# Attention and gated convolution FFN on one core: the last batch's copies get buffers of their own, and some twenty entries of the hand-written order move

## The chip, the cores and the metric

The kernel runs on one core of a Trainium2 chip. The metric is the device time of one execution in microseconds (us). Before the change it is 247.61 us, the median of three runs (248.05, 246.43 and 247.61).

The core has five engines that run side by side: TensorE (PE; its weight loads are shown as PEld), VectorE (DVE), ScalarE (ACT), GpSimd (POOL) and SyncE (SP). Matmuls write into PSUM, which DVE and ACT read; everything else lies in SBUF. Transfers are issued on the queues of SP or ACT and run on 16 DMA engines that all queues share.

## The reference

Eight batches of eight heads of causal attention, 576 positions of width 64, with a decay made of the running sum of logarithms; its output, 576 x 512 for each batch, goes through a feed-forward network of width 1024 whose hidden layer is gated by a convolution of three taps over the positions.

```python
def attn(q, k, v, f):                       # 8, 8, 576, 64; f: 8, 8, 576
    scores = q @ k.transpose(0, 1, 3, 2) / 8.0
    cum = np.cumsum(np.log(np.clip(f, 1e-4, 1.0)), axis=-1)
    scores = np.where(causal, -1e9, scores + cum[..., :, None] - cum[..., None, :])
    return softmax(scores) @ v

def ffn(x, w_in, conv_w, w_out):            # x: 8, 576, 512
    h = np.maximum(x @ w_in, 0.0)           # 8, 576, 1024
    gate = sigmoid(three_tap_conv_over_positions(h, conv_w))
    return (h * gate) @ w_out               # 8, 576, 512, float32
```

## The kernel before

**Tiling.** Attention works on half batches: hb 0 to 15, four heads each. For one hb the scores come in diagonal blocks (`sd`, two per hb), off-diagonal strips (`so`) and the last 64 positions (`st`). ACT turns each into exponentials (`ed`, `eo`, `et`), PE multiplies them by v (`pv`), DVE divides by the row sums (`n`, `m`), and the result is transposed (`t`, `tx`). After two half batches, batch b goes through the FFN in eight chunks ff of 128 hidden columns: `f` is the first matmul, `r` the ReLU on ACT, `c` and `d` the convolution on DVE, `a` the gate's function on ACT, `g` its product on DVE. The second matmul is `o`; `e` copies its PSUM tile into SBUF and `s` stores it.

**The last batch's output.** For b = 7 the second matmul is split by ff: `o7.c.ff` is one 128 x 128 by 128 x 512 matmul for position chunk c (0 to 4, of 128 positions). The last one for c is `o7.c.7`. Chunks 0 and 1 are the two halves of one PSUM tile of 128 x 1024, 2 and 3 the halves of another, 4 has a third. `e7.c` copies chunk c (line 485 before), `s7.c` stores it (line 491; chunk 4 in two pieces, lines 500 and 501). The copies of 0 and 1 go into the two halves of one SBUF tile `ob`, those of 2 and 3 into those of another, and the second of each pair is declared to come behind the first.

**The start.** The first two half batches are loaded plainly (`ld`) and transposed on PE (`tp`); `cl` then writes the transposed tile from PSUM to SBUF, on ACT or DVE. The others are loaded by transposing transfers (`q2.0` is q of half batch 2, `q2.1` its k). `ki` stores the decay rows to DRAM in three transfers, and `rw1`, `rw2` read some of them back into rows of the q and k tiles (lines 203 and 204, two small transfers each); the scores of that half batch wait for them. `wi0` to `wi3` load quarters of the first weight matrix (512 KB each), `wo0` to `wo3` those of the second, and `wic`, `woc` cast them. `v` loads values, `va` casts them. `cw` is a transpose of the convolution weights into PSUM, and `cwt` is seven small DVE instructions that read it (lines 298 to 305).

**What sets the order.** One list, `ORDER`, names every task, with `@` and an engine where there is a choice. `Plan.play` walks it and issues each task in turn, so each engine and each queue executes its own tasks in list order. Buffers are handed out in the same walk: `free[r].pop(0)` for a taker, `append` at the giver. There are four PSUM tiles (`ps`, numbered 129 to 132 in the program), so where in the list a task gives its tile back also decides which tile the later ones get. The recording layer adds the waits between engines. Each engine runs its instructions strictly in order, so that one that waits holds what stands behind it.

Of the kernel before, what the change touches and what calls it, by code (L numbers as in the profile page):

```python
# [21 lines left out]
class Plan:  # L22
# [34 lines left out]
def kernel(  # L57
# [11 lines left out]
    nc = tc.nc  # L69
# [36 lines left out]
    cw = cpool.tile([128, NFF, 3], FP32, name="cw")  # L106
    cwt = cpool.tile([128, NFF, 3], FP32, name="cwt")
# [316 lines left out]
    outf = out.rearrange("b s c -> (b s) c")  # L424
# [26 lines left out]
    def tanh(b, ff):  # L451
        nc.scalar.activation(hg_of(b, ff), u_t[slot[f"c{b}.{ff}", "u"]], AF.Sigmoid if (b, ff) in LATE else AF.Tanh, scale=cw[:, ff, 1:2])  # L452
# [11 lines left out]
    def shift(b):  # L464
        return 0 if low(b) == (b % 2 == 0) else S - 512
# [16 lines left out]
    def evac_chunk(b, c, e):  # L482
        j = c % 2
        o, i = ob_t[slot[f"e{b}.{c & ~1}", "ob"]][:, j, :], ps_of(f"o{b}.{c & ~1}.0")[:, 512 * j:512 * j + 512]
        (nc.scalar.copy if e == "ACT" else nc.vector.tensor_copy)(o, i)

    def store_chunk(b, c):
        if c == 4:
            return store(f"e{b}.4", b, c)
        r = b * S + shift(b) + 128 * c  # L490
        nc.sync.dma_start(outf[r:r + 128, :], ob_t[slot[f"e{b}.{c & ~1}", "ob"]][:, c % 2, :])

    def store(ev, b, c):
        ob, r = ob_t[slot[ev, "ob"]], b * S + shift(b) + 128 * c
        if c < 4:
            nc.sync.dma_start(outf[r:r + 256, :].rearrange("(j p) c -> p j c", p=128), ob)
        elif shift(b):
            nc.sync.dma_start(outf[b * S - SL:b * S + SL, :], ob[:, 0, :])
        else:
            nc.sync.dma_start(outf[b * S + 512:(b + 1) * S, :], ob[0:SL, 0, :])  # L500
            nc.sync.dma_start(outf[(b - 1) * S:(b - 1) * S + SL, :], ob[SL:128, 0, :])
# [35 lines left out]
    for hb in range(NHB):  # L537
        b = hb // 2
# [3 lines left out]
        if hb < NPL:  # L542
# [40 lines left out]
        for p in range(2):  # L583
            i = 2 * hb + p
# [34 lines left out]
    for b in range(B):  # L619
        last = b == B - 1  # L620
        for ff in range(NFF):
            add(f"f{b}.{ff}", "PE", [f"tx{2 * b}", f"tx{2 * b + 1}"] + [f"wic{2 * (ff // 4) + j}" for j in range(2)],
                lambda b=b, ff=ff: ffn1(b, ff), take=["ps"], behind=[f"f{b}.{ff - 1}"] if ff else [],
                give=[("xt", f"tx{2 * b}")] if ff == NFF - 1 else [])
            add(f"r{b}.{ff}", "ACT", [f"f{b}.{ff}"], lambda b=b, ff=ff: relu(b, ff), take=["ht"], give=[("ps", f"f{b}.{ff}")])
            add(f"c{b}.{ff}", "DVE", [f"r{b}.{ff}", "cwt"], lambda b=b, ff=ff: conv(b, ff, 0), take=["u"])
            add(f"d{b}.{ff}", "DVE", [f"c{b}.{ff}"], lambda b=b, ff=ff: conv(b, ff, 1))
            if ff == 0:
                add(f"h{b}", "ACT", [f"d{b}.{ff}"], lambda: None, take=["ho" if b % 2 else "he"])
            add(f"a{b}.{ff}", "ACT", [f"d{b}.{ff}"] + (["sgt"] if (b, ff) in LATE else []), lambda b=b, ff=ff: tanh(b, ff), give=[("u", f"c{b}.{ff}")],  # L630
                behind=[f"h{b}"])
            add(f"g{b}.{ff}", "DVE", [f"a{b}.{ff}"], lambda b=b, ff=ff: gate(b, ff), give=[("ht", f"r{b}.{ff}")])
        wo = [f"woc{j}" for j in range(4)]
        before = [f"g{b - 1}.{ff}" for ff in range(NFF)]
        if last:
            for ff in range(NFF):
                for c in range(NKB):
                    add(f"o{b}.{c}.{ff}", "PE", [f"g{b}.{ff}"] + (before if c == 4 and ff == 0 else []) + (wo if ff == 0 else []),
                        lambda b=b, c=c, ff=ff: ffn2(b, f"o{b}.{c & ~1}.0", c, [ff]),
                        take=["ps"] if ff == 0 and c % 2 == 0 else [],  # L640
                        behind=[f"o{b}.{c}.{ff - 1}"] if ff else [f"o{b}.{c - 1}.0"] if c % 2 else [])
        else:
            for c in range(4 + b % 2):
                a = c // 2
                first = f"o{b}.{2 * a}"
                add(f"o{b}.{c}", "PE", [f"g{b}.{ff}" for ff in range(NFF)] + (before if c == 4 else []) + wo,
                    lambda b=b, c=c, first=first: ffn2(b, first, c, range(NFF)), take=["ps"] if c % 2 == 0 else [],
                    behind=[f"o{b}.{c - 1}"] if c else [], give=[("he", f"h{b - 1}"), ("ho", f"h{b}")] if c == 4 else [])
        if last:
            for c in range(NKB):  # L650
                add(f"e{b}.{c}", "ACT/DVE", [f"o{b}.{c}.{NFF - 1}"], lambda e, b=b, c=c: evac_chunk(b, c, e),
                    take=["ob"] if c % 2 == 0 else [], behind=[f"e{b}.{c - 1}"] if c % 2 else [])
                add(f"s{b}.{c}", "SP", [f"e{b}.{c}"], lambda b=b, c=c: store_chunk(b, c))
            continue
        for a in range(2 + b % 2):
# [36 lines left out]
```

## Time and profile before

| | |
|---|---|
| median of three runs | 247.61 us (246.43 to 248.05) |
| the profiled execution | 246.53 us |
| its span, from the first to the last instruction | 244.8 us |
| PE busy | 226.9 us, 93% of the span |
| ACT, DVE, POOL busy | 206.8, 205.9, 51.5 us |
| granted TensorE clock | 0.999 of full speed |
| moved by DMA | 49.68 MB, 203 GB/s on average |

The span of the profiled execution is 1.73 us shorter than its own time. Busy shares are averages; PE's row also counts a modelled end for each matmul, and matmuls overlap. In the rows of the timeline the columns are start, duration, engine, line, operation, output and inputs, shapes and count, and in brackets how long the engine was idle before and what ended that. "SPq" and "ACTq" are the engines' issuing of transfers, not the transfers themselves.

### The profile page before, as it was taken

What the parts mean: (1) busy time and instruction counts of PE and PEld (TensorE: products, weight loads), DVE (VectorE), ACT (ScalarE), POOL (GpSimd) and SP (SyncE); (2) the same over time, 40 slices, a digit from 0 to 9 for tenths busy, and PEclk for the clock granted to TensorE, in tenths of its full rate; (3) what the DMA queues carried; (4) which work ended last, traced back from release to release, by engine and by line L of the source; (5) the groups of instructions that cost most, each with busy time, mean ns of one, the idle gap of its engine ahead of it and who ended that gap; (6) DMA issues with size and microseconds to landing.
All of it is one profiled execution on the core that took longest, in us unless ns stands there. A gap on an engine that the chain in (4) does not pass through costs nothing.

```text
span 244.8 us, 6395 instructions
## 1 busy us (share of the span) xinstructions
PE 226.9 (93%) x2627; PEld 145.2 (59%) x2627; DVE 205.9 (84%) x323; ACT 206.8 (84%) x278; POOL 51.5 (21%) x77
## 2 busy tenths in 40 slices
PE   0899799779989999999999999999999999999991
PEld 0787585557555676575556765685575566444440
DVE  5635359999998999999999979996999889999941
ACT  2768677999989899999999999999988996798442
POOL 8020520004220030022311580165302221000000
PEclk9999999999999999999999999999999999999999
DMA  7999999999899999999999999969997870541426
GB/s 189 333 162 243 289 212 197 196 249 260 187 178 177 222 162 246 252 297 208 195 251 264 202 189 274 263 144 186 240 255 192 210 165 3 146 162 58 163 86 214
DMA packets 120280, 49.68 MB, mean 203 GB/s; under 512 B 109863, under 2 KB 110375, under 8 KB 120251
## 3 DMA queue, kind: packets, MB, share of 16 engines
q1 hardware_dynamic: 120085, 48.97, 89.7%
q8 instruction: 20, 0.33, 0.6%
q10 hardware_dynamic: 166, 0.31, 0.4%
q14 instruction: 9, 0.07, 0.1%
HBM read 21.11 MB, written 10.17 MB: 128 GB/s over the span
## 4 chain that ended last, share of the span: by engine, by line
PE 80%; DVE 8%; DMA 6%; issue 1%; ACT 1%; POOL 1%; ACTq 1%; SPq 0%; DVEq 0%
PE ps L475 25%; PE ps L430 21%; PE ps L313 15%; PE ps L390 7%; PE ps L395 3%; PE ps L166 2%; PE ps L415 2%; PE ps L321 2%; DMA pd<-in_moe_conv_w_dram 2%; DMA ob<-in_moe_w_out_dram 2%; DVE u L447 2%; DVE u L449 2%; DMA qk<-image 2%; DVE hg L459 1%; DVE qk L186 1%
## 5 line engine op out<-in xcount | busy, mean ns | idle before, releaser
L430 PE MATMUL ps<-xt,w_in_f 128*128 128x512 f16 (+1 forms) x512 | 69.9, 286 | 0.0
L371 ACT ACTIVATE pp<-ps 128x1024 f16<-128x1024 f32 x64 | 64.8, 1033 | 4.4 <-PE ps L313 2.8
L475 PE MATMUL ps<-w_out_f,hg 128*128 128x512 f16 x288 | 66.9, 379 | 0.7 <-POOL w_out_f L519 0.7
L313 PE MATMUL ps<-qk 128*128 128x128 bf16 (+2 forms) x576 | 63.4, 240 | 1.6 <-DMA qk<-image 0.8
L447 DVE SCALAR_TENSOR_TENSOR u<-ht,cwt 128x576 f32<-128x576 f16 x64 | 53.3, 849 | 3.2 <-ACT ht L441 3.2
L452 ACT ACTIVATE hg<-u,cw 128x576 f16<-128x576 f32 x64 | 48.7, 784 | 5.9 <-DVE u L449 5.8
L449 DVE SCALAR_TENSOR_TENSOR u<-ht,cwt,u 128x576 f32<-128x576 f16 x64 | 53.1, 844 | 0.5
L430 PEld LDWEIGHTS <-w_in_f 128*128 128x128 f16 x512 | 34.4, 98 | 28.5
L313 PEld LDWEIGHTS <-qk 128*128 128x128 bf16 x576 | 39.2, 98 | 19.8 <-issue 3.0
L441 ACT ACTIVATE ht<-ps 128x576 f16<-128x576 f32 x64 | 40.9, 663 | 6.2 <-DVE hg L459 3.1
L475 PEld LDWEIGHTS <-hg 128*128 128x128 f16 x288 | 26.9, 98 | 29.7 <-issue 0.9
L459 DVE SCALAR_TENSOR_TENSOR hg<-hg,ht 128x576 f16<-128x576 f16 x51 | 39.0, 776 | 0.5 <-ACT hg L452 0.5
L357 POOL TENSOR_SCALAR_AFFINE_SELECT pp<-pd 128x1024 f16<-128x1024 f32 x16 | 19.7, 1244 | 51.7 <-ACT pd L354 51.7
L390 PE MATMUL ps<-va,pp 128*128 128x65 f16 x640 | 24.8, 193 | 1.0 <-DVE va L218 1.0
L390 PEld LDWEIGHTS <-pp 128*128 128x128 f16 x640 | 22.5, 97 | 3.5 <-DVE va L218 1.3
L406 DVE TENSOR_TENSOR xm<-ps,rc 128x896 f16<-128x896 f32 (+1 forms) x32 | 23.9, 751 | 0.5
L354 ACT ACTIVATE pp<-ps 128x1024 f16<-128x1024 f32 x16 | 16.6, 1038 | 5.2 <-PE ps L313 4.2
L354 ACT ACTIVATE pd<-ps 128x1024 f32<-128x1024 f32 x16 | 16.2, 1023 | 1.2 <-PE ps L313 1.0
L218 POOL CAST va<-vf 128x1024 f16<-128x1024 f32 x8 | 9.3, 1168 | 33.2 <-PE ps L415 18.5
L321 PE MATMUL ps<-mask,ident 128*128 128x512 bf16 (+1 forms) x40 | 14.3, 358 | 1.6 <-ACT pp L371 0.8
L404 DVE RECIPROCAL rc<-ps 128x14 f32<-128x14 f32 (+1 forms) x32 | 6.7, 209 | 9.8 <-PE ps L395 5.9
L480 ACT COPY ob<-ps 128x1024 f32<-128x1024 f32 (+1 forms) x14 | 12.9, 919 | 0.3 <-issue 0.2
(83 smaller groups left out, 176.2 us busy)
## 6 DMA issues: line engine op xcount, KB each, us to landing
vf<-in_v_dram SPq DMA_DIRECT2D x32, 256.0 KB
out_dram<-ob SPq DMA_DIRECT2D x14, 512.0 KB
qk<-blank SPq DMA_DIRECT2D x8, 432.0 KB
ob<-in_moe_w_in_dram SPq DMA_DIRECT2D x4, 512.0 KB
ob<-in_moe_w_out_dram SPq DMA_DIRECT2D x4, 512.0 KB
out_dram<-ob SPq DMA_DIRECT2D x6, 256.0 KB
vf<-in_v_dram SPq DMA_DIRECT2D x8, 128.0 KB
qk<-blank SPq DMA_DIRECT2D x8, 108.0 KB
```

The costliest lines, as they stand in the source:

```text
L313: nc.tensor.matmul(o, tk[:, h * S + k0:h * S + k0 + 128], tq[:, h * S + q0:h * S + q0 + n], start=first, stop=last and not by_matmul(hb, h))
L354: nc.scalar.activation(o, ps_of(f"sd{i}").rearrange("p (s c) -> p s c", s=2), AF.Exp, scale=SCALE)
L371: nc.scalar.activation(pair(i)[:, s, 512:1536], ps_of(f"so{i}.{s}"), AF.Exp, scale=SCALE)
L390: nc.tensor.matmul(ps[:, c:c + D + 1], block(hb, h, m, n), va[:, h, m, 0:D + 1], start=(m == 0), stop=(m == n))
L406: nc.vector.tensor_tensor(xm[:, CUT * D * u:CUT * D * u + nj * k * D].rearrange("p (j x d) -> p j x d", x=k, d=D), got[:, :, :, 0:D], r.un ...
L430: nc.tensor.matmul(ps[:, t0:t1], w_in_f16[:, cc, 128 * ff:128 * (ff + 1)], xt[:, cc // 2, x:x + t1 - t0], start=(cc == 0), stop=(cc == NCC ...
L441: nc.scalar.activation(ht_of(b, ff)[:, 2:2 + S], ps_of(f"f{b}.{ff}")[:, 0:S], AF.Relu, scale=1.0 if (b, ff) in LATE else 0.5)
L447: nc.vector.scalar_tensor_tensor(u, ht[:, 1:1 + S], cwt[:, ff, 0:1], ht[:, 2:2 + S], op0=ALU.mult, op1=ALU.add)
L449: nc.vector.scalar_tensor_tensor(u, ht[:, 3:3 + S], cwt[:, ff, 1:2], u, op0=ALU.mult, op1=ALU.add)
L452: nc.scalar.activation(hg_of(b, ff), u_t[slot[f"c{b}.{ff}", "u"]], AF.Sigmoid if (b, ff) in LATE else AF.Tanh, scale=cw[:, ff, 1:2])
L459: nc.vector.scalar_tensor_tensor(hv, hv, 1.0, ht_of(b, ff)[:, 2:2 + S], op0=ALU.add, op1=ALU.mult)
L475: nc.tensor.matmul(ps[:, 512 * (c % 2):512 * (c % 2 + 1)], w, w_out_f16[:, ff, :], start=(ff == 0), stop=(ff == NFF - 1))
```

## The change

There are two parts.

**The last batch's tail.** Chunks 1 and 3 are now copied into tiles of the pool `u`, which the convolution used; chunks 0, 2 and 4 keep an `ob` tile each. The declared order between the copies of a pair is gone. The store of chunk 2 is issued from ACT's queue instead of SP's. Chunk 0's copy is cut in two: `e7.0` copies columns 0 to 255 and a new task `eh7.0` columns 256 to 511, and its store waits for both.

**The order.** `q2.1` goes behind `ki`, and `wi3` moves ahead of both q2 loads. `cwt` goes from the start to a place behind `eo1.0`. Within q5 and within q6 the k load now precedes the q load. In the middle, `sd19`, `d3.4`, `r4.7`, `o4.1` and `d6.1` go a few places later in the list, and `va8.1` moves from DVE to POOL. At the end `o7.0.4` moves behind `o7.1.7` and `o7.1.7` ahead of `o7.0.5`, `e7.3` stands behind `o7.3.7` and `e7.1` behind `o7.0.4`. DVE copies chunks 4, 3 and 1 and the second half of 0, ACT copies 2 and the first half of 0; before, DVE copied 4 and 3 and ACT 2, 0 and 1.

```diff
-dca cw ld0 ... v0.4 va0.0@POOL va0.1@POOL q2.1 ki@SP cl0.0.0@ACT cl0.0.1@ACT cl0.1.0@ACT tp0.1.1 q2.0 cwt sd0 ed0 cl0.1.1@DVE wi1 wic1@POOL ... so1.0 st0 eo1.0 pv0.0
+dca cw ld0 ... v0.4 va0.0@POOL va0.1@POOL ki cl0.0.0@ACT cl0.0.1@ACT cl0.1.0@ACT tp0.1.1 wi3 q2.0 sd0 ed0 q2.1 cl0.1.1@DVE wi1 wic1@POOL ... so1.0 st0 eo1.0 cwt pv0.0
...
+    def last_out(b, c):
+        return u_t[slot[f"e{b}.{c}", "u"]] if c % 2 else ob_t[slot[f"e{b}.{c}", "ob"]][:, 0, :]
+
-    def evac_chunk(b, c, e):
-        j = c % 2
-        o, i = ob_t[slot[f"e{b}.{c & ~1}", "ob"]][:, j, :], ps_of(f"o{b}.{c & ~1}.0")[:, 512 * j:512 * j + 512]
+    def evac_chunk(b, c, e, n0=0, n1=512):
+        o, i = last_out(b, c)[:, n0:n1], ps_of(f"o{b}.{c & ~1}.0")[:, 512 * (c % 2) + n0:512 * (c % 2) + n1]
         (nc.scalar.copy if e == "ACT" else nc.vector.tensor_copy)(o, i)
...
-        nc.sync.dma_start(outf[r:r + 128, :], ob_t[slot[f"e{b}.{c & ~1}", "ob"]][:, c % 2, :])
+        (nc.scalar if c == 2 else nc.sync).dma_start(outf[r:r + 128, :], last_out(b, c)[:, 0:D_MODEL])
...
             for c in range(NKB):
-                add(f"e{b}.{c}", "ACT/DVE", [f"o{b}.{c}.{NFF - 1}"], lambda e, b=b, c=c: evac_chunk(b, c, e),
-                    take=["ob"] if c % 2 == 0 else [], behind=[f"e{b}.{c - 1}"] if c % 2 else [])
-                add(f"s{b}.{c}", "SP", [f"e{b}.{c}"], lambda b=b, c=c: store_chunk(b, c))
+                half = 256 if c == 0 else 512
+                add(f"e{b}.{c}", "ACT/DVE", [f"o{b}.{c}.{NFF - 1}"], lambda e, b=b, c=c, half=half: evac_chunk(b, c, e, 0, half),
+                    take=["u" if c % 2 else "ob"])
+                if c == 0:
+                    add(f"eh{b}.{c}", "ACT/DVE", [f"o{b}.{c}.{NFF - 1}"], lambda e, b=b, c=c: evac_chunk(b, c, e, 256, 512),
+                        behind=[f"e{b}.{c}"])
+                add(f"s{b}.{c}", "ACT" if c == 2 else "SP", [f"e{b}.{c}"] + ([f"eh{b}.{c}"] if c == 0 else []), lambda b=b, c=c: store_chunk(b, c))
```

What stands in the program after these edits is shown at three places.

First, SP's queue near the start, from the last load of the first values on; `qk_87` is the tile of half batch 2, `qk_86` that of half batch 1, and the `image` rows that write `qk` are `rw1` and `rw2`. Before:

```order
L210 DMA vf_89<-in_v_dram 64x8x64
L180 DMA_TRANSPOSE qk_87<-in_k_dram 128x2304
L280 DMA image<-kc 64x576 x3
L180 DMA_TRANSPOSE qk_87<-in_q_dram 128x2304
L511 DMA ob_125<-in_moe_w_in_dram 128x2x512
L203 DMA qk_86<-image 1x2304
L204 DMA qk_86<-image 2x2304
L511 DMA ob_126<-in_moe_w_in_dram 128x2x512
```

and after:

```order
L210 DMA vf_89<-in_v_dram 64x8x64
L280 DMA image<-kc 64x576 x3
L513 DMA ob_125<-in_moe_w_in_dram 128x2x512
L180 DMA_TRANSPOSE qk_87<-in_q_dram 128x2304
L180 DMA_TRANSPOSE qk_87<-in_k_dram 128x2304
L513 DMA ob_126<-in_moe_w_in_dram 128x2x512
L203 DMA qk_86<-image 1x2304
L204 DMA qk_86<-image 2x2304
```

The k transpose stands behind the three `image` stores, and one weight load more stands ahead of `rw1`.

Second, ACT's instructions on the PSUM tiles in the same stretch, with the tile's number: `ed0`, `eo0.1`, `eo0.0`, `cl1.0.0`, `ed1`, `cl1.1.1`, `eo1.1`. Before:

```order
L354 ACTIVATE pp0_95<-ps2_131 128x2x512
L371 ACTIVATE pp0_95<-ps3_132 128x1024
L371 ACTIVATE pp0_95<-ps2_131 128x1024
L172 ACTIVATE qk1_86<-ps0_129,lim_76 128x1152
L354 ACTIVATE pp1_96<-ps3_132 128x2x512
L172 ACTIVATE qk1_86<-ps0_129,lim_76 128x1152
L371 ACTIVATE pp1_96<-ps1_130 128x1024
```

and after:

```order
L354 ACTIVATE pp0_95<-ps2_131 128x2x512
L371 ACTIVATE pp0_95<-ps3_132 128x1024
L371 ACTIVATE pp0_95<-ps1_130 128x1024
L172 ACTIVATE qk1_86<-ps2_131,lim_76 128x1152
L354 ACTIVATE pp1_96<-ps1_130 128x2x512
L172 ACTIVATE qk1_86<-ps3_132,lim_76 128x1152
L371 ACTIVATE pp1_96<-ps1_130 128x1024
```

Tile 129, which `cw` holds until `cwt`, is not among them any more: the work turns on three tiles, and `ed1` (the fifth row) reads the tile that `eo0.0` (the third row) read, where before it read the one of `eo0.1` (the second row).

Third, the end of PE's queue with the waits that the recording layer put there: `o7.3.7`, `o7.2.7`, `o7.1.6`, `o7.1.7`, `o7.0.4`, `o7.0.5`, each with its weight load; tile 130 holds chunks 2 and 3, tile 132 chunks 0 and 1. After the change:

```order
L475 MATMUL ps1_130<-w_out_f16_70,hg_124 128x512
L475 LDWEIGHTS hg_124
L475 MATMUL ps1_130<-w_out_f16_70,hg_124 128x512 [waits DVE_49]
L475 LDWEIGHTS hg_124
L475 MATMUL ps3_132<-w_out_f16_70,hg_124 128x512
L475 LDWEIGHTS hg_124
L475 MATMUL ps3_132<-w_out_f16_70,hg_124 128x512
L475 LDWEIGHTS hg_124
L475 MATMUL ps3_132<-w_out_f16_70,hg_124 128x512
L475 LDWEIGHTS hg_124
L475 MATMUL ps3_132<-w_out_f16_70,hg_124 128x512 [waits DVE_49]
```

and DVE's copies of the chunks (4, 3, 1 and the half of 0), after:

```order
L487 COPY ob0_125<-ps0_129 128x512 [waits DMAHW6_49,DMAHW4_49,PE_49]
L487 COPY u2_122<-ps1_130 128x512 [waits PE_49]
L487 COPY u1_121<-ps3_132 128x512 [waits DVE_49,PE_49]
L487 COPY ob2_127<-ps3_132 128x256 [waits DMAHW7_49,DMAHW1_49,Activation_49]
L693 UNCONDITIONAL_BRANCH
```

where before there were two (4 and 3):

```order
L457 TENSOR_TENSOR hg_124<-hg_124,ht0_115 128x576 [waits PE_49,Activation_49]
L457 TENSOR_TENSOR hg_124<-hg_124,ht1_116 128x576 [waits PE_49]
L485 COPY ob3_128<-ps0_129 128x512 [waits DMAHW6_49,DMAHW4_49,PE_49]
L485 COPY ob2_127<-ps3_132 128x512 [waits DMAHW6_49,Activation_49]
L687 UNCONDITIONAL_BRANCH
```

In the list after the change `e7.3` stands ahead of `o7.2.7` and `e7.1` ahead of `o7.0.5`, and those two matmuls, which write the other half of the tile that the copy reads, wait for DVE. Before, no matmul behind `o7.4.7` waits for anything. The wait of chunk 3's copy for ACT is gone, and the half copy of chunk 0 waits for ACT.

2 lines of the change are left out of this document (1 added, 1 removed).

## The prediction

> **What bounds the kernel now.** I read first a table by stage: the busy time of each engine in four stretches, with the DMA share and rate in the last two columns.
>
> ```profile
> 8.20:25.00 16.80, 16.80 (x212) 14.31 (x213) 9.60 (x16) 13.60 (x13) 1.37 (x2) 1.00 1.15 239
> 25.00:71.00 46.00, 40.72 (x548) 27.55 (x545) 37.93 (x57) 40.40 (x55) 11.32 (x11) 1.00 1.06 226
> 71.00:239.60 168.60, 168.44 (x1866) 102.40 (x1865) 153.87 (x232) 149.37 (x207) 33.42 (x34) 1.00 0.85 192
> 239.60:244.80 5.20, 0.07 (x1) 0.00 (x0) 0.38 (x1) 1.07 (x2) 0.00 (x0) 0.94 0.70 235
> ```
>
> The columns after the length are PE, PEld, DVE, ACT, POOL, granted clock. From 71.0 to 239.6 PE is busy for 168.44 of 168.60 us at the full clock. Nothing can be won there by moving other engines' work; an edit can only open a gap. From 25 to 71 PE idles for 46.0 - 40.7 = 5.3 us, and 5.2 us follow the last matmul. So the two ends decide. The waits of PE between, from the list of who waited for whom, and four pieces of the chain that ended last:
>
> ```profile
> PE ps L390 <- DVE va L218: 1.0, 1, 1.0
> PE ps L313 <- DMA qk<-image: 0.8, 1, 0.8
> PE ps L475 <- POOL w_out_f L519: 0.7, 1, 0.7
> ```
>
> ```profile
> 22.51 3.80 DMA qk<-image
> 26.36 0.40 PE ps L313 x4
> ...
> 64.27 5.08 DMA ob<-in_moe_w_out_dram
> 69.40 1.70 POOL w_out_f L519
> ```
>
> PE's first wait on the way is 0.8 us for `rw1`, the small read behind a full DMA queue that lands 3.80 us after its issue at 22.51; its last is 0.7 us for a weight cast whose load landed late, before 71.1.
>
> **The tail, step by step.** The last six matmuls and the four copies around them, then the three rows that price a half copy and a restart of PE:
>
> ```profile
> 238.21 1.46 PE L475 MATMUL ps<-w_out_f,hg 128*128 128x512 f16 x6
> ...
> 237.33 0.69 DVE L485 COPY ob<-ps 128x512 f32<-128x512 f32 x1 [2.10 <-PE ps L475]
> 238.67 0.58 ACT L485 COPY ob<-ps 128x512 f32<-128x512 f32 x1 [3.40 <-issue]
> 239.28 0.69 DVE L485 COPY ob<-ps 128x512 f32<-128x512 f32 x1 [1.26 <-ACT ob L485]
> 239.70 1.07 ACT L485 COPY ob<-ps 128x512 f32<-128x512 f32 x2 [0.45 <-PE ps L475]
> ```
>
> ```profile
> L475 PE MATMUL ps<-w_out_f,hg 128*128 128x512 f16 x288 | 66.9, 379 | 0.7 <-POOL w_out_f L519 0.7
> 24.40 0.38 ACT L333 ACTIVATE pt<-ps 128x256 f16<-128x256 f32 x1 [0.33 <-PE ps L318]
> 32.09 0.42 DVE L406 TENSOR_TENSOR xm<-ps,rc 128x256 f16<-128x256 f32 x1
> 27.23 1.02 ACT L354 ACTIVATE pp<-ps 128x1024 f16<-128x1024 f32 x1 [2.44 <-PE ps L313]
> 28.31 0.60 PE L313 MATMUL ps<-qk 128*128 128x64 bf16 x4 [0.45 <-ACT pp L354]
> ```
>
> Matmuls start every (1.46 - 0.38) / 5 = 0.216 us; the first of the six is `o7.2.7`, at 238.21, the last `o7.0.7`, at 239.29. The copies that wait for them start 0.46 and 0.41 us later (238.67, 239.70); I take 0.42. PE starts again 28.31 - 28.25 = 0.06 us after an ACT instruction that held it. Chunk 4's copy at 237.33 puts `o7.4.7` at 236.91.
>
> What goes: chunk 3's copy no longer waits for chunk 2's (1.26 us), chunk 1's no longer follows chunk 0's on ACT. What comes are waits of PE for DVE, at `o7.2.7` and `o7.0.5`; behind each stands all that PE has left. In the new order:
> - `o7.3.7` is the fourth after `o7.4.7`: 236.91 + 4 x 0.216 = 237.77. `e7.3` runs from 238.19 to 238.88. `o7.2.7`, due at 237.99, starts at 238.94: 0.95 us lost.
> - `e7.2` on ACT from 239.36 to 239.94; its store is issued there.
> - `o7.1.6`, `o7.1.7`, `o7.0.4` at 239.16, 239.37, 239.59. `e7.1`, which waits for PE, runs from 240.01 to 240.70. `o7.0.5`, due at 239.80, starts at 240.76: 0.96 us lost. `o7.0.7` starts at 241.19, 1.9 us later than before.
> - The half copy `e7.0` at 241.61, 0.38 us, to 241.99; then `eh7.0` on DVE, which waits for ACT, 0.42 us, to 242.47. Its store is issued at 242.50.
>
> The halves cost 0.06 + 0.38 + 0.42 = 0.86 us in a row, where one copy takes 0.58. [...]
>
> Before, the last store was issued at 240.9, and the rates show when the data had left, against a store that stood alone:
>
> ```profile
> L491 SPq DMA_DIRECT2D out_dram<-ob x4: 351/409/524, 239.3 to 240.9; - x4
> L496 SPq DMA_DIRECT2D out_dram<-ob x1: 372/372/372, 235.3 to 235.3; - x1
> ```
>
> ```profile
> 236.00:237.00 1.00, 1.00 (x6) 0.48 (x5) 0.00 (x0) 0.00 (x0) 0.00 (x0) 1.00 0.82 309
> 237.00:238.00 1.00, 1.00 (x7) 0.41 (x6) 0.67 (x1) 0.00 (x0) 0.00 (x0) 1.00 0.58 215
> 241.00:242.00 1.00, 0.00 (x0) 0.00 (x0) 0.00 (x0) 0.00 (x0) 0.00 (x0) 1.00 0.92 342
> 242.00:243.00 1.00, 0.00 (x0) 0.00 (x0) 0.00 (x0) 0.00 (x0) 0.00 (x0) 1.00 1.04 385
> 243.00:244.00 1.00, 0.00 (x0) 0.00 (x0) 0.00 (x0) 0.00 (x0) 0.00 (x0) 1.00 0.35 131
> ```
>
> The stores queued at 385 GB/s until 243 + 131 / 385 = 243.35, 2.4 us after the last issue. The lone store of 524 KB, issued at 235.3, moved 309 KB before 237, so at that rate it began 0.8 us before 237, at 236.2: 0.9 us after its issue. Now the last 262 KB stand alone: 242.50 + 0.9 + 262 / 385 = 244.1, which is 0.75 us later. If a first byte takes 1.2 us, it is 1.05. The row nearest is the lone store; since the last one also has ACT's store ahead of it I take **+0.9**. Bounds: +0.3 (the halves overlap, 0.48 less) and +1.05.
>
> **The head.** `cwt` now keeps its PSUM tile, so `sd1` takes the tile that `eo0.0` reads.
>
> ```profile
> 17.45 0.38 PE L321 MATMUL ps<-mask,ident 128*128 128x512 bf16 x1
> ...
> 17.15 1.02 ACT L371 ACTIVATE pp<-ps 128x1024 f16<-128x1024 f32 x1 [0.79 <-PE ps L318]
> 18.07 1.30 ACT L172 ACTIVATE qk<-ps,lim 128x1152 uint16<-128x1152 uint16 x1
> 19.42 1.02 ACT L354 ACTIVATE pp<-ps 128x1024 f16<-128x1024 f32 x1
> 20.43 1.31 ACT L172 ACTIVATE qk<-ps,lim 128x1152 uint16<-128x1152 uint16 x1
> ```
>
> `sd1` started at 17.45; it now waits for 18.17 + 0.06: 0.78 us. `ed1` (19.42) then starts near 20.2 and `cl1.1.1`, on which `rw1` waits, ends near 22.5 instead of 21.74. `so1.1` waits for `ed1` another 0.25 us, so PE comes to `sd2` about 1.0 us later, where 0.94 us of idle time (its wait of 0.8 with the matmul ahead of it) stood: at 26.45 against 26.36. The seven instructions of `cwt`, 1.3 us, now lie between DVE's casts:
>
> ```profile
> 10.47 0.18 DVE L298 COPY cw<-ps 128x24 f32<-128x24 f32 x1
> 11.63 0.17 DVE L305 TENSOR_TENSOR cwt<-cw,cwt 128x8 f32<-128x8 f32 x1
> 19.05 0.28 DVE L220 CAST va<-vf 64x256 f16<-64x256 f32 x1
> 20.00 1.48 DVE L174 TENSOR_SCALAR qk<-ps,lim 128x1152 uint16<-128x1152 uint16 x1 [0.68 <-PE ps L166]
> ```
>
> From 19.33 to 20.65 they stand ahead of `cl1.1.0` (20.00), which PE, 0.78 us late, holds to 20.8 in any case; it ends at 22.3, before 22.5: nothing more. Then `rw1` needs its landing. `wi3`, 524 KB, now stands ahead of it: at the stage's 226 GB/s 2.3 us. Against that, DMA engines were nearly idle where `q2.1` stood:
>
> ```profile
> 17.00:18.00 1.00, 1.00 (x18) 0.88 (x16) 0.34 (x1) 0.85 (x1) 0.83 (x2) 1.00 0.07 7
> 20.00:21.00 1.00, 1.00 (x15) 0.71 (x12) 1.00 (x1) 1.00 (x2) 0.00 (x0) 1.00 0.60 132
> ```
>
> 7 and 132 KB instead of 226 are 1.4 us of room. If `wi3` fills it, `rw1` lands 2.3 - 1.4 = 0.9 us later; the bounds are 0 (PE is late anyway) and 2.3. I take 0.9. The bytes up to `wo2` are the same, so that load is not later, and the 0.7 us for which PE waited for it take up most: **+0.2** at 71 us, between -0.7 (no wait left there) and 2.3 - 0.7 = +1.6.
>
> **The middle.** The swaps within q5 and q6 exchange equal transfers; `sd19`, `o4.1`, `d3.4`, `r4.7`, `d6.1` change places with work that PE has queued; `va8.1` takes one small cast (0.28 us in the row at 19.05) off DVE. PE is full there, so 0; a gap that one opens would be as long as the matmul group displaced, which I leave to the range.
>
> **Sum.** 246.53 + 0.9 + 0.2 = 247.6 us for the profiled execution. The median of the runs is 247.61, 1.1 above it, so the forecast is **248.6 us**.
>
> **Rivals.**
> - Slower: `wi3` fills no hole, and `rw1` lands the full 2.3 us later. It decides from 0.8 us on, where PE's slack at 70 us ends. For it: the hole lies where a transposing load had just been issued, and these loads still stand there. Against: the two loads are now back to back. Time: 247.61 + 0.9 + 1.6 = 250.1. Chance 0.13.
> - Faster: the stream of transfers moves up by its 1.4 us of holes, and the waits of 1.0 (value cast) and 0.7 (weight cast) go. For it: in 8 to 71 us DMA is the fullest resource (1.15, 1.06). Against: the cast on DVE stood in a queue of DVE work, not for a transfer. 247.61 + 0.9 - 1.7 = 246.8. Chance 0.2.
> - The two matmuls do not wait long, because DVE comes sooner than I think. Then `e7.1` runs from 239.06, `e7.0` from 239.70, the last half ends at 240.6 and the stores, no longer in one bunch, end about 0.3 us sooner: 247.61 - 0.3 + 0.2 = 247.5. Against it: each copy can start only when its own last matmul is done. Chance 0.15.
> - My forecast: 0.52. That the copies still wait for each other, against the words of the change, is part of it.
>
> **Chances.** About 1% (2.5 us) is what a measurement of this kernel can tell from no change; the runs shown spread over 1.6. Below 245.1 no case reaches by itself: 0.05. Above 250.1: half of the first rival and the upper end of the forecast, 0.11. Within: 0.84. The range for 8 in 10 goes from the faster rival to the slower one, 246.8 to 250.1.
>
> **What would show it.** Right: two gaps of PE of about 0.95 us among the last nine matmuls, each ended by a DVE copy; the half copy on DVE behind ACT's; the last store issued about 1.3 us after `o7.0.7` starts, with no queue ahead of it; a wait of PE of 0.8 us near 17.5 and `sd2` between 26.4 and 27.3. Wrong: no gap at the tail; `rw1` landing past 27.5; a wait of PE between 71 and 237 us; or a PE that reaches 71 us work more than 0.7 us early.

## The result, and the profile after

The changed kernel takes 248.68 us (median of 22 runs, 247.42 to 251.38) against 247.24 us for the kernel before in as many (245.69 to 249.23). The ratio is 1.0064, with a 95% interval from 1.0040 to 1.0088: 1.6 us slower, with an interval from 1.0 to 2.2. The ratios, here and below, leave out executions that lie more than 1.5% above the fastest of their kernel (here the one of 251.38), so that they differ a little from the ratio of the medians. The forecast was 248.6 us, within 0.1 us of the median, and the measured time lies in its range. The profiled execution is one of the longest: 250.91 us, span 249.2, 4.4 us longer than that of before. Its trace shows what goes wrong, but too large for the median. Experiments 2 and 4 have the same start, experiment 7 the same but for `cwt`; their traced executions (247.04, 246.57 and 246.64 us) are among the quicker ones of their kernels, and PE waits 1.46, 0.91 and 1.35 us for `rw1` in them. An execution near the median was not traced.

The longest wait of PE in the changed kernel is the one at its very start, 7.0 us (7.3 before). The next two in the list (total, times, longest) stood at 0.8 us and nowhere before:

```profile
PE ps L313 <- DMA qk<-image: 3.4, 1, 3.4
PE ps L475 <- DVE u L487: 1.6, 2, 0.8
```

The first is the wait for `rw1`, the second the two at the tail. The weight cast `woc2`, for which PE waited 0.7 us near 70 us before, is not in the list.

**The tail.** The end of the timeline of the changed kernel:

```profile
236.64 5.34 PE L475 MATMUL ps<-w_out_f,hg 128*128 128x512 f16 x24
...
242.02 0.69 DVE L487 COPY u<-ps 128x512 f32<-128x512 f32 x1 [0.17 <-PE ps L475]
...
242.77 1.02 PE L475 MATMUL ps<-w_out_f,hg 128*128 128x512 f16 x4 [0.78 <-DVE u L487]
...
243.83 0.69 DVE L487 COPY u<-ps 128x512 f32<-128x512 f32 x1 [1.11 <-PE ps L475]
...
244.57 0.81 PE L475 MATMUL ps<-w_out_f,hg 128*128 128x512 f16 x3 [0.78 <-DVE u L487]
...
245.41 0.37 ACT L487 COPY ob<-ps 128x256 f32<-128x256 f32 x1 [1.60 <-PE ps L475]
245.82 0.42 DVE L487 COPY ob<-ps 128x256 f32<-128x256 f32 x1 [1.30 <-ACT ob L487]
246.27 0.33 SPq L493 DMA_DIRECT2D out_dram<-ob  x1
```

The matmul before `o7.2.7` starts at 236.64 + 5.34 - 0.38 = 241.60; `o7.2.7` was due 0.216 later and starts at 242.77, 0.95 us late. In the same way `o7.0.5` is due at 243.63 and starts at 244.57, 0.94 us late. Each wait ends with a copy on DVE that reads the other half of the tile. The last matmul starts at 244.57 + 0.81 - 0.38 = 245.00, against 239.29: 5.7 us later, of which 1.9 is the tail and 3.8 came from ahead.

**The start.** SP's queue, and what PE did:

```profile
14.94 0.60 SPq L513 DMA_DIRECT2D ob<-in_moe_w_in_dram  x1
15.58 5.50 SPq L180 DMA_TRANSPOSE qk<-in_q_dram  x1
21.13 2.51 SPq L180 DMA_TRANSPOSE qk<-in_k_dram  x1
23.69 0.59 SPq L513 DMA_DIRECT2D ob<-in_moe_w_in_dram  x1
...
24.81 0.69 SPq L204 DMA_DIRECT2D qk<-image  x1
```

```profile
17.81 0.38 PE L321 MATMUL ps<-mask,ident 128*128 128x512 bf16 x1 [0.61 <-ACT pp L371]
...
25.82 0.38 PE L321 MATMUL ps<-mask,ident 128*128 128x512 bf16 x1
29.62 0.61 PE L313 MATMUL ps<-qk 128*128 128x128 bf16 x4 [3.43 <-DMA qk<-image]
...
35.76 0.41 PE L390 MATMUL ps<-va,pp 128*128 128x65 f16 x8
```

In the kernel before, the same load, and a later one that there stood behind `wi3`:

```profile
18.98 2.23 SPq L180 DMA_TRANSPOSE qk<-in_q_dram  x1
...
26.20 5.51 SPq L180 DMA_TRANSPOSE qk<-in_q_dram  x1
```

`q2.0`, now right behind `wi3`, keeps SP busy for 5.50 us; before it took 2.23. Of the five entries ahead of `rw1`, `q2.0` thus takes 3.27 us more and `wi3` adds 0.60, while `q2.1` and `ki` take 0.64 and 0.53 less, and the first of them starts 0.24 us sooner. The second transfer of `rw1` is issued at 24.81 instead of 22.51, and in this execution it also lands later after its issue, 4.77 us instead of 3.80:

```profile
24.81 4.77 DMA qk<-image
```

The two together, 2.30 and 0.97 us, make up the delay of `sd2`, which starts at 29.62 instead of 26.36, 3.3 us late. By the matmul group that before stood at 30.97 (below) and now stands at 35.76, the delay is 4.8 us: 1.5 us more, though nothing waits for a transfer there. The table of short stretches, with the clock ahead of the last two columns, tells why:

```profile
28.10:28.20 0.10, 0.00 (x0) 0.00 (x0) 0.00 (x0) 0.00 (x0) 0.00 (x0) 0.90 0.63 246
28.20:28.30 0.10, 0.00 (x0) 0.00 (x0) 0.00 (x0) 0.00 (x0) 0.00 (x0) 0.50 0.82 266
...
35.00:35.10 0.10, 0.10 (x2) 0.00 (x0) 0.00 (x0) 0.09 (x1) 0.00 (x0) 0.96 0.25 59
```

The matmul group in the timeline of the kernel before:

```profile
30.97 0.41 PE L390 MATMUL ps<-va,pp 128*128 128x65 f16 x8
```

While PE waited, the granted clock fell to half, and it stayed there until 35.0, 5.4 us after PE had work again. At 0.50 the eight matmuls of L313 that start at 30.45 took 1.49 us; the same eight at 26.81 in the kernel before, at 1.00, took 0.82.

### The profile page after: what moved, and what is told of

The parts are those of the page before. It is cut to its first block, busy times and chain, and to the rows that moved or that the text cites. A ratio compares the mean times of both kernels' runs of the same rounds, so it can differ in the third digit from the quotient of the medians.

```text
span 249.2 us, 6398 instructions
## 1 busy us (share of the span) xinstructions
PE 229.7 (92%) x2627; PEld 146.4 (59%) x2627; DVE 207.6 (83%) x324; ACT 206.5 (83%) x277; POOL 52.0 (21%) x78
## 4 chain that ended last, share of the span: by engine, by line
PE 82%; DVE 9%; DMA 4%; ACT 2%; issue 1%; ACTq 0%; DVEq 0%
PE ps L475 25%; PE ps L430 22%; PE ps L313 17%; PE ps L390 7%; PE ps L321 3%; PE ps L395 2%; PE ps L415 2%; DVE u L447 2%; DMA u<-in_f_dram 2%; DMA qk<-image 2%; DVE u L449 2%; DVE qk L186 1%; PE ps L316 1%; PE ps L318 1%; ACT qk L172 1%
## 5 line engine op out<-in xcount | busy, mean ns | idle before, releaser
L313 PE MATMUL ps<-qk 128*128 128x128 bf16 (+2 forms) x576 | 65.4, 245 | 4.2 <-DMA qk<-image 3.4
L313 PEld LDWEIGHTS <-qk 128*128 128x128 bf16 x576 | 40.5, 100 | 23.2 <-issue 4.2
L459 DVE SCALAR_TENSOR_TENSOR hg<-hg,ht 128x576 f16<-128x576 f16 x51 | 40.3, 803 | 0.2 <-ACT hg L452 0.2
L357 POOL TENSOR_SCALAR_AFFINE_SELECT pp<-pd 128x1024 f16<-128x1024 f32 x16 | 19.1, 1210 | 53.6 <-ACT pd L354 53.6
L390 PEld LDWEIGHTS <-pp 128*128 128x128 f16 x640 | 22.5, 97 | 3.7 <-DVE va L218 1.5
L218 POOL CAST va<-vf 128x1024 f16<-128x1024 f32 x8 | 10.1, 1264 | 32.9 <-DMA vf<-in_v_dram 32.9
L321 PE MATMUL ps<-mask,ident 128*128 128x512 bf16 (+1 forms) x40 | 15.1, 380 | 1.6 <-ACT pp L371 1.1
L186 DVE TENSOR_SCALAR qk<-qk,lim 128x2304 uint16<-128x2304 uint16 x12 | 11.5, 971 | 3.1 <-DMA qk<-in_q_dram 1.6
```

The costliest lines, as they stand in the source:

```text
L313: nc.tensor.matmul(o, tk[:, h * S + k0:h * S + k0 + 128], tq[:, h * S + q0:h * S + q0 + n], start=first, stop=last and not by_matmul(hb, h))
L390: nc.tensor.matmul(ps[:, c:c + D + 1], block(hb, h, m, n), va[:, h, m, 0:D + 1], start=(m == 0), stop=(m == n))
L459: nc.vector.scalar_tensor_tensor(hv, hv, 1.0, ht_of(b, ff)[:, 2:2 + S], op0=ALU.add, op1=ALU.mult)
```

## The experiments

Each kernel was timed in five rounds beside the kernel before on the same chip, whose median was 246.0 to 246.4 us; ratios are to it, with 95% intervals. Most have twelve executions, experiment 2 has eight and experiment 6 six, and one execution of each was traced. For scale, 0.1% is 0.25 us.

**1. The tail alone.** The tail's code of the change, and of its order only what stands behind `o7.4.7`:

```diff
-... o7.4.7 o7.0.4 o7.3.6 o7.1.5 o7.2.6 e7.4@DVE e6.1@ACT o7.3.7 s6.1 o7.2.7 e7.2@ACT o7.1.6 o7.0.5 e7.3@DVE o7.0.6 o7.1.7 o7.0.7 s7.4 s7.2 s7.3 e7.0@ACT s7.0 e7.1@ACT s7.1
+... o7.4.7 o7.3.6 o7.1.5 o7.2.6 e7.4@DVE e6.1@ACT o7.3.7 e7.3@DVE s6.1 o7.2.7 e7.2@ACT s7.2 o7.1.6 o7.1.7 o7.0.4 e7.1@DVE o7.0.5 o7.0.6 o7.0.7 s7.4 s7.3 s7.1 e7.0@ACT eh7.0@DVE s7.0
```

> The kernel before, with the change's tail alone (its buffers, its queue for chunk 2, its cut of chunk 0, and its order behind `o7.4.7`); start and middle as before. Theory: the two matmuls `o7.2.7` and `o7.0.5` wait 0.95 us each for a DVE copy, the last matmul is 1.9 us later, and the stores end sooner after it; the trace of the changed kernel has 3.8 us from the last matmul to the end of the span where before had 5.1, so +1.9 - 1.3 = +0.6 us over the kernel before; the prediction's term was +0.9 (0.3 to 1.05). Rival: the stores' queue sets the end whatever PE does, so the stalls are free and the time is that of before or 0.3 less.

Measured: 1.0027 (1.0003 to 1.0051), +0.7 us. The theory holds: the stalls, 1.9 us by the same working as above, reach the end, but not in full. The last matmul and the last bytes of the stores:

```profile
241.10 0.81 PE L475 MATMUL ps<-w_out_f,hg 128*128 128x512 f16 x3 [0.78 <-DVE u L487]
...
242.80 0.33 SPq L493 DMA_DIRECT2D out_dram<-ob  x1
```

```profile
242.00:243.00 1.00, 0.00 (x0) 0.00 (x0) 0.42 (x1) 0.31 (x1) 0.00 (x0) 1.00 0.98 367
...
244.00:245.00 1.00, 0.00 (x0) 0.00 (x0) 0.00 (x0) 0.00 (x0) 0.00 (x0) 1.00 0.33 121
```

The last matmul starts at 241.53 and the bytes are out at 244 + 121 / 367 = 244.33, 2.80 us later; before it was 243.35 - 239.29 = 4.06. So 1.26 of the 1.9 us that PE loses come back behind the last matmul, where the stores no longer queue. The last store is issued at 242.80 and its bytes are out 1.53 us later, where before it was 2.4.

**2. The start alone.** The order of the change up to the loads of q3:

```diff
-... v0.4 va0.0@POOL va0.1@POOL q2.1 ki@SP ... tp0.1.1 q2.0 cwt sd0 ed0 cl0.1.1@DVE wi1 ... eo1.0 pv0.0 ... wi2 wic0@POOL wi3 et1 ...
+... v0.4 va0.0@POOL va0.1@POOL ki ... tp0.1.1 wi3 q2.0 sd0 ed0 q2.1 cl0.1.1@DVE wi1 ... eo1.0 cwt pv0.0 ... wi2 wic0@POOL et1 ...
```

> The kernel before, with the change's order up to the loads of q3 alone (place of `ki`, `wi3`, the two q2 loads and `cwt`); middle and tail as before. Prediction's term: +0.2 (-0.7 to +1.6), with `rw1` 0.9 us later. Theory after the trace of the changed kernel: `rw1` is issued 2.3 us later, PE waits some 3.4 us for it instead of 0.8, the granted clock falls to 0.5 behind that wait, and the time is +0.8 to +1.2 in the median and up to +3 in single executions. Rival: the changed kernel's long wait belongs to its profiled execution only; then +0.2 and a PE wait under 2 us here.

Measured: 1.0074 (1.0040 to 1.0107), +1.8 us, single executions up to 249.43. The head by itself is clearly slower, by more than the 0.8 to 1.2 us of the theory. The profiled execution is a milder one (247.04 us, where the median is 248.03). It has the slow issue, but not the low clock (1.00 from 25 to 38 us), and its wait of 1.46 us is, as the rival expected, under 2:

```profile
15.16 0.59 SPq L511 DMA_DIRECT2D ob<-in_moe_w_in_dram  x1
15.79 4.81 SPq L180 DMA_TRANSPOSE qk<-in_q_dram  x1
...
24.46 0.69 SPq L204 DMA_DIRECT2D qk<-image  x1
```

```profile
27.99 0.40 PE L313 MATMUL ps<-qk 128*128 128x128 bf16 x4 [1.46 <-DMA qk<-image]
```

`sd2` is 1.6 us late, and of that 0.8 us is regained near 70 us, where the weights no longer arrive too late (the matmuls that stood at 69.44 are 1.45 us late, those of 72.44 only 0.61). A wait of 3.4 us and the clock that falls behind it are thus not in every execution. `rw1` is issued here only 0.35 us sooner than in the changed kernel, but it lands 3.49 us after its issue, where there it took 4.77; the trace does not show why. Nor is it shown what makes the long executions in general. Of the seven of the changed kernel at 249.8 us and more, the mean granted clock is 0.981 in the traced one and 0.991 to 0.993 in four; in the other two, of which one is the longest of all (251.38), it is 0.997 and 0.999 (an estimate: 3.41 us at half clock, as in experiment 6, would take 0.007 off), so that the clock is not what made these long.

**3. The middle alone.**

```diff
-... eo7.0 q5.0 va3.0@ACT a0.4 f0.6 q5.1 ... va8.1@DVE ...
+... eo7.0 va3.0@ACT a0.4 f0.6 q5.1 q5.0 ... va8.1@POOL ...
```

(and the other single moves between the loads of q3 and `o7.4.7`.)

> The kernel before, with the change's order from the loads of q3 to `o7.4.7` alone (the swaps in q5 and q6, `sd19`, `d3.4`, `r4.7`, `o4.1`, `d6.1`, `va8.1` on POOL). Theory: PE has work queued there and each swap is neutral: 0, within 0.3 us. Rival: the moves feed PE sooner between 25 and 71 us, where it idles 5.3 us before: 0.5 to 0.8 us less.

Measured: 0.9999 (0.9973 to 1.0025). No effect is seen, as forecast; the interval (-0.7 to +0.6 us) just reaches the smaller gain of the rival. The three parts add up to 1.0% against the 0.64% of the whole; with intervals of 0.25 to 0.35% each, that is not a contradiction.

**4. The changed kernel without PE's waits.**

```diff
-... o7.3.7 e7.3@DVE s6.1 o7.2.7 e7.2@ACT s7.2 o7.1.6 o7.1.7 o7.0.4 e7.1@DVE o7.0.5 o7.0.6 o7.0.7 s7.4 ...
+... o7.3.7 s6.1 o7.2.7 e7.3@DVE e7.2@ACT s7.2 o7.1.6 o7.1.7 o7.0.4 o7.0.5 o7.0.6 o7.0.7 e7.1@DVE s7.4 ...
```

> The changed kernel, with `e7.3` placed behind `o7.2.7` and `e7.1` behind `o7.0.7` in the list, so that no matmul is told to wait for a copy; all else as changed. Theory: the two stalls of 0.95 us go, the last matmul comes 1.9 us sooner, the last copy ends some 1.5 us behind it, and the time is 0.7 to 1.2 us under that of the changed kernel. Rival: the stores' queue then sets the end as it did before, and less than 0.3 us is won.

Measured: 1.0063 (1.0036 to 1.0091), where the changed kernel has 1.0064: the gain that was expected is not seen. The waits are gone from its trace. But this kernel keeps the changed start, and its executions scatter from 246.26 to 249.95 us; the two intervals are 0.6 to 0.7 us to each side, and a gain of 0.7 us can hide in them. So the same edit was made on the quiet start (experiment 9).

**5. `wi3` back.**

```diff
-... tp0.1.1 wi3 q2.0 sd0 ed0 q2.1 ... wi2 wic0@POOL ...
+... tp0.1.1 q2.0 sd0 ed0 q2.1 ... wi2 wi3 wic0@POOL ...
```

> The changed kernel, with `wi3` alone put back behind `wi2`; the q2 loads still stand behind `ki`, one behind the other. Theory A: a transposing load that stands right behind a 512 KB weight load is slow to issue (5.5 us for `q2.0` in the changed kernel, 2.2 us in the kernel before), so with `wi3` gone from there `q2.0` issues in 2 to 3.3 us, `rw1` is issued at 21.5 to 22.5 instead of 24.8, PE's wait for it is that of the kernel before (0.8 to 1.3), and the time falls by 0.8 to 1.0 us to that of the tail alone. Theory B: it is the two transposing loads in a row that hold SP's queue; then `q2.0` still takes about 5 us, `rw1` is issued near 24, PE waits 1.5 us or more, and the time falls by 0.3 us at most.

Measured: 1.0042 (1.0018 to 1.0067); 0.5 us under the changed kernel by the ratios, where A forecast 0.8 to 1.0, and within their intervals, so that the times alone do not show what `wi3` costs. For the issue the trace decides:

```profile
15.69 2.20 SPq L180 DMA_TRANSPOSE qk<-in_q_dram  x1
17.94 3.92 SPq L180 DMA_TRANSPOSE qk<-in_k_dram  x1
...
23.13 0.31 SPq L203 DMA_DIRECT2D qk<-image  x1
```

`q2.0` issues in 2.20 us although `q2.1` still follows directly. For the issue theory A holds and theory B falls. Among the eight longest waits of PE in this run there is none for `rw1` any more. `rw1` goes out later than A said, 23.62 instead of 22.5 for its second transfer, because SP now stands idle ahead of it (22.49 to 23.13), until the copy `cl1.1.0` on DVE ends at 23.10. That copy starts at 21.62, behind transposes that the wait at `sd1` has put off: here it is the place of `cwt` that sets when `rw1` is issued.

**6. `q2.1` back.**

```diff
-... va0.1@POOL ki ... wi3 q2.0 sd0 ed0 q2.1 ...
+... va0.1@POOL q2.1 ki ... wi3 q2.0 sd0 ed0 ...
```

> The changed kernel, with `q2.1` alone put back ahead of `ki`; `wi3` stays ahead of `q2.0`. Theory A (the weight load ahead stretches the issue): `q2.0` still takes about 5 us, `q2.1` 3 us, `rw1` is issued near 24.5 or later, and nothing is won. Theory B (two transposing loads in a row): both issue in 2.2 to 3.3 us, `rw1` is issued near 23 (0.6 us more than before, for `wi3`), PE's wait is 0.8 to 1.5 us, and 0.6 to 0.8 us are won.

Measured: 1.0125 (1.0089 to 1.0161), twice the loss of the changed kernel.

```profile
14.19 2.67 SPq L180 DMA_TRANSPOSE qk<-in_k_dram  x1
...
19.70 0.60 SPq L513 DMA_DIRECT2D ob<-in_moe_w_in_dram  x1
20.35 4.73 SPq L180 DMA_TRANSPOSE qk<-in_q_dram  x1
...
26.30 0.69 SPq L204 DMA_DIRECT2D qk<-image  x1
```

The two transposing loads are apart, and the one behind `wi3` still takes 4.73 us: theory A again. `rw1` is issued 3.8 us later than in the kernel before, and PE waits 2.1 us:

```profile
29.42 0.40 PE L313 MATMUL ps<-qk 128*128 128x128 bf16 x4 [2.13 <-DMA qk<-image]
```

So with `wi3` ahead of `q2.0`, the move of `q2.1` behind `q2.0` makes the kernel faster, by 0.6%. Without `wi3` there it changes little: experiment 5 has 1.0042, the tail alone 1.0027. That points to the move of `wi3` as the harmful one.

**7. `cwt` back.**

```diff
-... q2.0 sd0 ... eo1.0 cwt pv0.0 ...
+... q2.0 cwt sd0 ... eo1.0 pv0.0 ...
```

> The changed kernel, with `cwt` alone put back to its early place, so that its PSUM tile is free again. Theory: PE's wait of 0.78 us at `sd1` goes, and the wait for `rw1` grows by as much, since its issue is set by SP's queue at 24 to 25 us; the time is that of the changed kernel within 0.3 us. Rival: the wait at `sd1` delays the copies on which `rw1` depends and so the start of `sd2`; then 0.6 to 0.8 us are won.

Measured: 1.0061 (1.0029 to 1.0093): no change is seen, though with these intervals a gain of the rival's 0.6 to 0.8 us cannot be excluded. PE's list of waits in its trace has 1.3 us for `rw1` and no wait at `sd1`. That fits the theory: the 0.78 us that `cwt`'s place costs at `sd1` lies hidden ahead of the wait for `rw1`.

**8. `rw1` ahead of `wi1`,** in the kernel before with the neutral middle:

```diff
-... cl0.1.1@DVE wi1 wic1@POOL so0.1 ... cl1.1.0@DVE rw1 sd2 ...
+... cl0.1.1@DVE so0.1 ... cl1.1.0@DVE rw1 wi1 wic1@POOL sd2 ...
```

> The kernel before, with the middle of the change (neutral in its own run) and `wi1` with its cast moved behind `rw1`; tail and the rest of the start as before. Theory: `rw1` no longer waits for `wi1` (0.75 us of issue and 512 KB), lands 0.8 to 2 us sooner, PE's wait at `sd2` goes, and 0.5 to 0.8 us are won against the kernel before. Rival: PE's next waits (1.0 us for a cast of values near 48, and the weight casts near 70) take it back, and the time is that of before within 0.3 us.

Measured: 1.0006 (0.9982 to 1.0030). The wait at `sd2` goes, and PE is 1.1 us early at 26 us; then it waits 1.49 us at 32.5 for `rw2`, which stands behind all four weight loads, as it did before:

```profile
32.54 0.40 PE L313 MATMUL ps<-qk 128*128 128x128 bf16 x4 [1.49 <-DMA qk<-image]
```

The rival is right in its time, with another wait than the ones it named. That the one wait turned into the other is not shown by this trace alone: in experiment 1, where the start is that of before, PE also waits for `rw2` and not for `rw1`:

```profile
33.32 0.40 PE L313 MATMUL ps<-qk 128*128 128x128 bf16 x4 [1.29 <-DMA qk<-image]
```

In experiments 9 and 10, with the same start, it waits 0.30 and 0.86 us there.

**9. The tail alone without PE's waits:** the edit of experiment 4 on the kernel of experiment 1.

> The kernel before, with the change's tail alone, and in it `e7.3` placed behind `o7.2.7` and `e7.1` behind `o7.0.7`, so that no matmul waits; to be read against the run of the tail as it is. Theory: the data of the last store leave about 0.7 us sooner than with the waits (in the traces so far 4.0 us after the last matmul's start of the kernel before, against 4.7 with the waits), so 0.6 to 0.7 us under the tail as it is, and level with the kernel before within 0.2. Rival: the change's tail costs by its cut of chunk 0 and its three copies in a row on one PSUM tile, waits or not; then it is as slow as the tail as it is, +0.5 or more over the kernel before.

Measured: 0.9987 (0.9957 to 1.0017), against 1.0027 with the waits: 0.4%, 1.0 us less (a difference of two ratios with intervals of 0.24 and 0.30%), and level with the kernel before.

```profile
235.83 4.48 PE L475 MATMUL ps<-w_out_f,hg 128*128 128x512 f16 x20
...
241.07 0.37 ACT L487 COPY ob<-ps 128x256 f32<-128x256 f32 x1 [0.67 <-DVE u L487]
241.47 0.42 DVE L487 COPY ob<-ps 128x256 f32<-128x256 f32 x1 [0.44 <-ACT ob L487]
```

```profile
242.00:243.00 1.00, 0.00 (x0) 0.00 (x0) 0.00 (x0) 0.00 (x0) 0.00 (x0) 1.00 1.03 389
243.00:244.00 1.00, 0.00 (x0) 0.00 (x0) 0.00 (x0) 0.00 (x0) 0.00 (x0) 0.83 0.91 336
```

The last matmul starts at 235.83 + 4.48 - 0.38 = 239.93, and the bytes are out at 243 + 336 / 389 = 243.86, 3.93 us later. With the waits it is 1.88 + 2.80 = 4.68 counted from the same point: 0.75 us less. The three copies of tile `o7.0` and `o7.1` still follow each other, `e7.0` behind `e7.1` and `eh7.0` behind `e7.0`.

**10. Chunk 0 copied whole,** in the kernel of experiment 1:

```diff
-                half = 256 if c == 0 else 512
+                half = 512
...
-... e7.0@ACT eh7.0@DVE s7.0
+... e7.0@ACT s7.0
```

> The kernel before, with the change's tail alone, but chunk 0 copied whole by ACT instead of in two halves; the two waits of PE stay. Theory: the two halves followed each other (0.37 + 0.42 us and the steps between them, 0.83 in all, against 0.58 for a whole copy), so the last store is issued 0.25 to 0.3 us sooner and the time is 0.2 to 0.3 us under the tail as it is. Rival: the halves cost nothing or the end hangs on another store; then no difference within 0.1 in the trace.

Measured: 1.0016 (0.9989 to 1.0042), 0.3 us under experiment 1, as expected but within the intervals. The trace agrees:

```profile
240.20 0.81 PE L475 MATMUL ps<-w_out_f,hg 128*128 128x512 f16 x3 [0.78 <-DVE u L487]
241.05 0.58 ACT L487 COPY ob<-ps 128x512 f32<-128x512 f32 x1 [1.61 <-PE ps L475]
241.66 0.33 SPq L493 DMA_DIRECT2D out_dram<-ob  x1
```

The store is issued 1.03 us after the last matmul's start at 240.63; with the halves it was 242.80 - 241.53 = 1.27. In these traces the cut costs 0.24 us and gains nothing.

**11. `rw1` and `rw2` ahead of the weights:** experiment 8 with `wi2` and `wi3` behind `rw2`.

```diff
-... st1 wi0 so2.0 sd3 wi2 wic0@POOL wi3 et1 eo2.0 cl2.0 cl2.1 rw2 n0.0 ...
+... st1 wi0 so2.0 sd3 wic0@POOL et1 eo2.0 cl2.0 cl2.1 rw2 wi2 wi3 n0.0 ...
```

> The kernel before, with the middle of the change, and `rw1` ahead of `wi1`, `rw2` ahead of `wi2` and `wi3`. Theory: PE's waits for both pairs of rows go (in the run with `rw1` alone moved the wait of 0.8 us at 26 became one of 1.5 us for `rw2` at 32), PE comes to 48 us 0.8 to 1.1 us sooner than in the kernel before, and 0.3 to 0.8 us are won at the end. Rival: the weights, which now land later, hold PE at the first feed-forward matmul or at the weight loads near 70 us, and the time is that of before within 0.3 us.

Measured: 1.0023 (0.9996 to 1.0050). Not won. The row waits at 26 and 32 us are gone from its trace, and PE is 1.3 us ahead until 43; there it waits 1.50 us for the next rows, `rw3`:

```profile
44.89 0.38 PE L313 MATMUL ps<-qk 128*128 128x128 bf16 x4 [1.50 <-DMA qk<-image]
```

The rival is right in its time, but the wait that takes the gain back is not one of those it named: `rw3` is issued at 41.03 instead of 39.87, behind loads that come later now. Here what one set of rows wins, the next gives back. No version tried is faster than the kernel before by more than its interval.

## Why the prediction was right, and where it was not

- **The two stalls of PE:** forecast 0.95 and 0.96 us, in the trace 0.95 and 0.94, each ended by the copy that was named. Right, mechanism and size.
- **The half copies in a row:** 0.06 + 0.38 + 0.42 = 0.86 us forecast; from 245.41 to 246.24 it is 0.83. Right, and the whole copy shows what it costs (0.24 us, experiment 10). Whether the halves could run side by side is not shown: in every run that has them the second waits for the first.
- **The tail's term:** forecast +0.9 (0.3 to 1.05), measured +0.7 alone. The step from the last issue to the last byte was 242.50 to 244.1, 1.6 us; measured 1.53. In the prediction's sum 1.15 of the 1.9 us lost at PE come back (the end moves by 0.75); in the trace 1.26 did. The upper bound's 1.2 us to a first byte is shown by no run: 1.53 us less 262 KB at 367 GB/s leave 0.8.
- **The middle:** 0 forecast, 0.9999 measured.
- **`cwt`'s tile:** a wait of 0.78 us at `sd1` was forecast; the matmul starts at 17.81, after the exponential of `eo0.0`, where by the row ahead of it, 0.42 us earlier than before, it was due at 17.03. It lies ahead of the wait for `rw1`, and no cost is seen at the end (experiment 7), as said.
- **The weight load near 70 us:** the forecast let PE's wait of 0.7 us there take up that much of the delay. The wait is gone from the list, and in experiment 2 0.8 us of the delay are regained there. Right.
- **The head's term is the step that failed:** +0.2 (-0.7 to +1.6) was forecast, +1.8 measured alone, and 0.9 by the difference of the whole and the tail. The step was "If `wi3` fills it, `rw1` lands 2.3 - 1.4 = 0.9 us later". It does not fill the hole. The holes of before stood at 17 and 20 us, when SP was issuing or had just issued a transposing load, and in the changed kernel the rate is low from 16 to 21 us, while SP issues `q2.0`; between the two rows shown here (GB/s in the last column) it is 205, 171 and 155:

```profile
16.00:17.00 1.00, 1.00 (x16) 0.91 (x14) 0.00 (x0) 0.27 (x1) 1.00 (x2) 1.00 0.54 94
...
20.00:21.00 1.00, 0.89 (x18) 0.77 (x16) 0.86 (x3) 1.00 (x2) 0.00 (x0) 1.00 0.58 99
```

  From 13 to 22 us 1.7 MB are moved in either kernel, `wi3` ahead of `rw1` or not. That `wi3` fills no hole is the condition of the slower rival, although its time of 250.1 us did not come. The prediction weighed `wi3` by its bytes; in the traces its price is the longer issue of the load behind it. A like price stood in the trace of before, at 26.20, where a transposing load behind `wi3` and two small row reads took 5.51 us to issue.
- **A sign of being wrong came:** the prediction named "`rw1` landing past 27.5". It landed at 24.81 + 4.77 = 29.58 in the changed kernel and at 24.46 + 3.49 = 27.95 in experiment 2, and `sd2` started at 29.62, outside the 26.4 to 27.3 of the forecast. How much of the +1.8 us of the head's median is the later issue, the slower landing and the clock is not shown.
- **The clock** was not in the prediction at all. In the profiled execution 1.5 us of the delay arise while it is low.
- **The sum** lies closer to the measurement than its terms do. The base of the forecast was the median of three runs, 247.61; that of 22 is 247.24, 0.4 less. With the tail 0.2 smaller, that makes room for a start that is 0.7 to 1.6 us dearer. That the forecast lies within 0.1 us of the median is luck. Against the kernel before, +1.0 was forecast and +1.6 measured.

The rival with short waits of PE and the faster one are refuted: the waits have the forecast length, and of the two waits that the faster one would have saved, that for the value cast grew from 1.0 to 1.3 us, while that for the weight cast went because PE came later.

## What to carry to other kernels

A transfer that is moved in a queue can also change how long the instructions next to it take to issue (2.20 us for `q2.0` without `wi3` ahead of it, 5.50 with it); look up what that pair costs elsewhere in the trace before counting bytes. A wait that the tracking of whole tiles puts on a matmul can be removed by placing the copy behind the matmuls of the same tile (experiment 9), and a copy cut in two gained nothing here, where the halves follow each other (0.83 us against 0.58 for the whole). Where several small transfers share one queue with large ones, hurrying the first did not win time: PE then waited 1.49 and 1.50 us for the next (experiments 8 and 11).

## What the runs showed of the hardware that was not expected

**Issue of transposing loads.** On SP's queue the loads of q2 took 2.20 to 3.92 us to issue where no weight load stands directly ahead (the two kernels and experiments 2, 4 to 8 and 11; but 4.52 and 4.49 for `q2.1` in experiments 8 and 11, behind a load of values), and 4.21 to 5.50 us right behind a 512 KB weight load (5.50 in the changed kernel, 4.81, 4.69, 4.73 and 4.21 in experiments 2, 4, 6 and 7). With the weight load taken away, the same load took 2.20 us at the same time (experiment 5). What in the queue makes it so, the trace does not show.

**The clock.** In the changed kernel PE's last matmul before the wait ends at 25.82 + 0.38 = 26.20, and the clock falls at 28.18 (28.1 and the part of 0.1 us that makes a mean of 0.90), after 1.98 us of idleness; it is back at 35.01, 6.83 us later. In experiment 6 PE idles from 27.30 to 29.42, 2.12 us, and the clock falls only at 30.68, when PE has been at work for 1.3 us; it is back at 34.09, 3.41 us later:

```profile
30.50:30.70 0.20, 0.20 (x5) 0.19 (x4) 0.00 (x0) 0.20 (x1) 0.20 (x2) 0.94 1.22 266
30.70:30.80 0.10, 0.10 (x5) 0.10 (x4) 0.00 (x0) 0.10 (x1) 0.10 (x1) 0.50 0.90 307
...
34.00:34.10 0.10, 0.10 (x4) 0.10 (x2) 0.00 (x0) 0.00 (x0) 0.10 (x1) 0.56 1.26 287
```

6.83 is twice 3.41. A wait of 1.46 us (experiment 2) did not bring the clock down. At the end of the changed kernel the clock falls once more, at 246.63:

```profile
246.60:246.70 0.10, 0.00 (x0) 0.00 (x0) 0.00 (x0) 0.00 (x0) 0.00 (x0) 0.67 0.03 0
```

PE's last matmul there ended at 245.38, only 1.25 us ahead of that fall; with the wait of 0.78 us ahead of `o7.0.5` it idled 2.03 of the 2.84 us before it. In the kernel before PE's last matmul ended at 239.66 and the clock fell at 244.15, 4.49 us later. So the length of the last gap alone does not set when the clock falls; what does, these traces do not show. What makes the low stretch 3.41 us in one run and 6.83 in another, no run here shows either, and the two executions above 249.8 us with a mean clock of 0.997 and 0.999 show that the clock is not the whole of the scatter.
